# A diffusion-transformer block on one core: the MLP gate's cross-partition sum by small DMAs, and the place of two scale groups in the K stage

## The chip, the cores and the metric

The kernel runs on one core of a Trainium2 chip. The metric is the device time of one execution in microseconds; the median of five runs is compared. One execution was taken with the hardware profiler, and its trace is what the views below are read from. Engines are named as in the profile: PE is TensorE's matmul, PEld its weight load, DVE is VectorE, ACT ScalarE, POOL GpSimd, SP the engine that issues most of the loads.

## The reference

One block of a diffusion transformer for x of shape (2, 256, 1152), in bfloat16, with a conditioning vector c per batch. Six vectors of 1152 elements per batch are made from c: shift, scale and gate for the attention half, and the same for the MLP half.

```
mod = (silu(c) @ w_mod).reshape(B, 6, 1, D)
shift_a, scale_a, gate_a, shift_m, scale_m, gate_m = mod[:, 0..5]
h   = layernorm(x) * (1 + scale_a) + shift_a
q, k, v from h @ wqkv, 2 heads of 576
a   = softmax(q k^T / sqrt(576)) v @ wo
x   = x + gate_a * a
h2  = layernorm(x) * (1 + scale_m) + shift_m
m   = gelu(h2 @ w_fc1) @ w_fc2          # 1152 -> 4608 -> 1152
out = x + gate_m * m
```

## The kernel before

The 512 tokens (2 batches of 256) are the free dimension of most matmuls, and D = 1152 is cut into KD = 9 chunks of 128 partitions, F = 4608 into KF = 36. All engines run their instructions in the order of the program: the last lines of the kernel chain the instructions of each engine in that order, so a step's place in the text is its place in the engine's queue. Weights stream in by large DMAs from SP into five wide buffers, and each is released when its last reader is done.

**K stage.** The keys come first. The modulated input hT0 is made chunk by chunk: `scale_group(k0, k1)` multiplies columns of w_scale_a with silu(c) on PE (line 250, tile pm), `scale_add` adds one on VectorE (line 260), `transpose_x` turns a chunk of the normalised input over on PE (line 267, tile pt), and `both` (line 319) multiplies the chunk with its scale: batch 0 on VectorE (line 273), batch 1 on ScalarE (line 274). `k_step(k, c0, c1, m0, m1)` then adds chunk k to the accumulators of panels m0 to m1 of six panels of K (line 282), for token columns c0 to c1. w_scale_a is loaded in five pieces (line 109), interleaved with pieces of w_k (line 106): chunks 0-1, 2-3, 4-5, 6-7 and 8. The loop from chunk 3 on (lines 400 to 409) does, at k = 3 and k = 5, the first three panels of step k, then the scale group of the next two chunks, then the transposes of chunk k + 1, and then the other panels of step k. Steps 4 and 6 go in two halves of 256 tokens, batch 0 first. The two PSUM buffers of tag aux hold pm and pt in turn. After the K stage come the other three K panels, shift_a, the q panels, scores and softmax, V, the attention product, the output projection with gate_a, and the second layernorm.

**The MLP gate.** gate_m is needed only at the very end, as a row broadcast to all partitions. `gate_vector` makes it on VectorE while PE runs fc1: after panel 22, VectorE multiplies each of the nine chunks of w_gate_m with silu(c) (lines 472 and 474), and adds them up in part, 128 partitions by 1152 per batch. What is left is a sum over the 128 partitions. VectorE transposes in blocks of 32 by 32 (line 481) and sums each block along the free dimension (line 482): folded holds, for each of the four quadrants of 32 partitions, the sum of that quadrant. The sum over the four quadrants goes by matmul: `gate_vector_finish` (line 488), called behind panel 34, multiplies folded with fold, a constant of four stacked identities, in float32, one matmul per batch (line 492, tile pg; four instructions in the profile). VectorE casts the result (line 494), POOL writes it to a DRAM scratch (line 496), and reads it back broadcast over the partitions (`broadcast_gate`, line 461).

**fc1 and fc2.** fc1 has 36 panels: the first 12 in halves of 256 tokens, the others with nine matmuls of 512 columns each (line 751), with a Gelu on ScalarE behind each (lines 772 and 783). fc2 follows with thirteen groups of 36 matmuls (line 807), most of 384 columns, in a pool of six PSUM accumulators. Behind each group VectorE multiplies with gate_m (line 813), POOL (in the last group VectorE) adds the residual (line 815), and SP stores the output (line 818).

Of the kernel before, what the change touches and what calls it, by code (L numbers as in the profile page):

```python
# [8 lines left out]
FP32 = mybir.dt.float32  # L9
BF16 = mybir.dt.bfloat16  # L10
ACT = mybir.ActivationFunctionType
ALU = mybir.AluOpType
AX = mybir.AxisListType
# [6 lines left out]
def kernel(  # L20
# [11 lines left out]
    nc = tc.nc  # L32
    B, N, D = x.shape
# [3 lines left out]
    P = 128  # L37
    T = B * N
# [3 lines left out]
    KF = F // P  # L42
# [10 lines left out]
    const = ctx.enter_context(tc.tile_pool(name="const", bufs=1))  # L53
    act = ctx.enter_context(tc.tile_pool(name="act", bufs=1))
    wide = ctx.enter_context(tc.tile_pool(name="wide", bufs=5))
    work = ctx.enter_context(tc.tile_pool(name="work", bufs=2))
    small = ctx.enter_context(tc.tile_pool(name="small", bufs=4))
    psum = ctx.enter_context(tc.tile_pool(name="psum", bufs=2, space=PSUM))

    def acc_tile(shape, name, dt=FP32):  # L60
        return psum.tile(shape, dt, name=name, tag="acc", bufs=6)

    def aux_tile(shape, name, dt=FP32):
        return psum.tile(shape, dt, name=name, tag="aux", bufs=2)
# [27 lines left out]
    ident = const.tile([P, P], BF16, name="ident")  # L92
# [26 lines left out]
    def load_rows(name, view, col0):  # L119
        w = wide_tile(name)  # L120
        for r in range(0, KD, 3):
            load = nc.sync.dma_start(w[:, r:r + 3, :], view[:, r:r + 3, col0:col0 + D])
            first_load.setdefault(name, load.ins)
        return w
# [118 lines left out]
    def scale_group(k0, k1, tile_of=aux_tile, pm=None):  # L243
        if pm is None:
            pm = tile_of([P, k1 - k0, B], "pm")
        for j in range(k0, k1):
            if j == 0:
                nc.tensor.matmul(pm[:, 0, :], ones_row[:], ones_row[:, 0:B], start=True, stop=False)
            for k in range(KD):
                nc.tensor.matmul(  # L250
                    pm[:, j - k0, :], w_scale_a[:, k, j * P:(j + 1) * P], sT[:, k, 0:B],
                    start=(k == 0 and j > 0), stop=(k == KD - 1),
                )
        return pm

    def scale_add(pm, k0, k1, eng="d"):
        if eng == "a":
            nc.scalar.activation(scale_a[:, k0:k1, :], pm[:], ACT.Identity, bias=ones[:])
        else:
            nc.vector.tensor_scalar_add(scale_a[:, k0:k1, :], pm[:], 1.0)  # L260

    def transpose_x(ks, ts, pt=None, j0=0):
        if pt is None:
            pt = aux_tile([P, len(ks), len(ts) * P], "pt", BF16)
        for j, t in enumerate(ts, j0):
            for i, k in enumerate(ks):
                nc.tensor.transpose(pt[:, i, j * P:(j + 1) * P], xns[t][:, k * P:(k + 1) * P], ident[:])  # L267
        return pt
# [9 lines left out]
    def k_step(k, c0=0, c1=T, m0=0, m1=KM1):  # L278
        for m in range(m0, m1):
            if k == 0 and c0 == 0:  # L280
                pk[m] = acc_tile([P, T], "pk")
            nc.tensor.matmul(  # L282
                pk[m][:, c0:c1], w_k[:, k, m * P:(m + 1) * P], hT0[:, k, c0:c1],
                start=(k == 0 and c0 == 0), stop=(k == KD - 1), skip_group_check=True,
            )
# [33 lines left out]
    def both(pt, k):  # L319
        for b, e in enumerate("da"):  # L320
            modulate(pt, 0, k, b, b * N, e)
# [76 lines left out]
    k_step(2, 0, N)  # L398
    k_step(2, N, T)
    for k in range(3, KD):  # L400
        split = 3 if k in (3, 5) else 0
        k_step(k, 0, T, 0, split)
        if k in (3, 5, 7):
            k1 = min(k + 3, KD)
            scale_add(scale_group(k + 1, k1), k + 1, k1)
        if k < KD - 1:
            both(transpose_x([k + 1], range(NT)), k + 1)
        for c0, c1 in ((0, N), (N, T)) if k in (4, 6) else ((0, T),):
            k_step(k, c0, c1, split)
    for m in range(KM1):  # L410
        k_evac(m)

# [38 lines left out]

    s32 = const.tile([P, KD, B], FP32, name="s32")
    nc.vector.tensor_copy(s32[:], sT[:, :, 0:B])
    fold = const.tile([P, 32], FP32, name="fold")
    nc.vector.tensor_reduce(fold[:], ident[:].rearrange("p (q a) -> p a q", a=32), axis=AX.X, op=ALU.add)
    gates_dram = tc.dram_tile([2, B, D], BF16, name="gates_dram")

    def broadcast_gate(g):
        gate = act.tile([P, B, D], BF16, name="gate", tag="gate")
        for b in range(B):  # L460
            nc.gpsimd.dma_start(gate[:, b, :], gates_dram[g, b:b + 1, :].partition_broadcast(P))
        return gate
# [3 lines left out]
    def gate_vector(g, wg):  # L466
        part = act.tile([P, B, D], FP32, name="part", tag="x_sb")
        folded = small.tile([P, B, D // 32], FP32, name="folded", tag="folded", bufs=1)
        for k in range(KD):
            for b in range(B):  # L470
                if k == 0:
                    nc.vector.tensor_scalar_mul(part[:, b, :], wg[:, k, :], s32[:, k, b:b + 1])  # L472
                else:
                    nc.vector.scalar_tensor_tensor(  # L474
                        part[:, b, :], wg[:, k, :], s32[:, k, b:b + 1], part[:, b, :],
                        op0=ALU.mult, op1=ALU.add,
                    )
        for b in range(B):
            for c in range(0, D, PW):
                blocks = work.tile([P, PW // 32, 32], FP32, name="tmp", tag="tmp", bufs=3)  # L480
                nc.vector.transpose(blocks[:].rearrange("p j r -> p (j r)"), part[:, b, c:c + PW])
                nc.vector.tensor_reduce(
                    folded[:, b, c // 32:(c + PW) // 32], blocks[:], axis=AX.X, op=ALU.add
                )

        return lambda: gate_vector_finish(g, folded)

    def gate_vector_finish(g, folded):
        rows = D // 32
        pg = aux_tile([rows, B, 32], "pg")  # L490
        for b in range(B):
            nc.tensor.matmul(pg[:, b, :], folded[:, b, :], fold[:], start=True, stop=True)
        nat = work.tile([rows, B, 32], BF16, name="nat_v", tag="nat_v", bufs=1)
        nc.vector.tensor_copy(nat[:], pg[:])  # L494
        for b in range(B):
            nc.gpsimd.dma_start(gates_dram[g, b, :].rearrange("(j r) -> j r", r=32), nat[:, b, :])  # L496
        return broadcast_gate(g)

    def gate_natural(g, wg):
# [130 lines left out]
    w_gate_m = load_rows("w_gate_m", wmod_v, S_GATE_M * D)  # L630
# [106 lines left out]
    def load_f2(j):  # L737
        w = wide.tile([P, 27, PW], BF16, name=f"w_f2_{j}", tag="wide")
        i = 27 * j
        while i < 27 * (j + 1):  # L740
            n, kk = divmod(i, KF)
            cnt = min(KF - kk, 27 * (j + 1) - i)
            nc.sync.dma_start(w[:, i - 27 * j:i - 27 * j + cnt, :], wfc2_v[:, kk:kk + cnt, n * PW:(n + 1) * PW])
            i += cnt
        w_f2.append(w)
# [3 lines left out]
    def f1_mm(dst, m, k, c0, c1, start, **kw):  # L749
        ml = m % KD  # L750
        nc.tensor.matmul(  # L751
            dst, w_f1[m // KD][:, k, ml * P:(ml + 1) * P], hT[:, k, c0:c1],
            start=start, stop=(k == KD - 1), **kw,
        )
# [23 lines left out]
    gate_m = None  # L778
    for m in range(MSPLIT, KF):
        pacc = acc_tile([P, T], "pacc")  # L780
        for k in range(KD):
            f1_mm(pacc[:], m, k, 0, T, k == 0)
        nc.scalar.activation(gT[:, m, :], pacc[:], ACT.Gelu_apprx_tanh)  # L783
        if m == 22:
            gate_m_finish = gate_vector(1, w_gate_m)
        if m == KF - 2:
            gate_m = gate_m_finish()
        if m == MSPLIT:
            load_f2(0)
        if m > MSPLIT and m % KD == KD - 1:  # L790
            load_f2(m // KD)
# [9 lines left out]
    for gi, (n, t, c0, cw) in enumerate(groups):  # L801
        b = t // TPB
        last = gi == len(groups) - 1
        pacc = acc_tile([P, cw], "pacc")
        for kk in range(KF):
            j, r = divmod(n * KF + kk, 27)
# [3 lines left out]
                start=(kk == 0), stop=(kk == KF - 1),  # L810
# [51 lines left out]
```

## Time and profile before

| | |
|---|---|
| median of five runs | 243.28 us (242.82 to 243.54) |
| the profiled execution's own time | 243.54 us |
| its span | 241.8 us |
| granted TensorE clock | 1.0 |
| PE busy | 235.1 us, 97% of the span |
| DVE, ACT, POOL busy | 91.5, 60.2, 28.3 us |
| share of the chain that ended last | PE 94%, DMA 3% |

The span is the time from the first to the last instruction in the trace; the time of an execution is 1.74 us longer. In the timeline, each line gives start and duration in microseconds, the engine, the line of the kernel, the operation, output and input tiles, shapes and the number of instructions merged; in brackets stands how long the engine was idle before, and what ended the idle time. In the chain that ended last, each line gives start, duration, engine, tile, line and number of instructions. A few per cent of the matmul records can be missing from a trace, so a count may be short by one.

### The profile page before, as it was taken

The page shows a single profiled execution, that of the slowest core. Times are in us where ns is not written, and L with a number is a line of the kernel's source. Part 1 is how long each engine was busy: PE and PEld are TensorE (multiplying, and loading weights), DVE is VectorE, ACT ScalarE, POOL GpSimd, SP SyncE. Part 2 cuts the span into 40 slices and gives each one's busy share as a digit, 9 for nine tenths or more (in the row PEclk, how much of TensorE's full clock was granted, in tenths as well). Part 3 has the DMA queues.
Part 4 walks back from the last instruction along what each step waited for, and adds up shares of the span by engine and source line. Part 5 has one row for each costly group of instructions (what it writes and reads, how often), then busy time and mean ns, then how long its engine had stood idle before and what let it go on. Part 6 is the DMA issues. An engine that isn't in the chain of part 4 may idle for free.

```text
span 241.8 us, 4006 instructions
## 1 busy us (share of the span) xinstructions
PE 235.1 (97%) x1699; PEld 145.4 (60%) x1710; DVE 91.5 (38%) x194; ACT 60.2 (25%) x122; POOL 28.3 (12%) x47
## 2 busy tenths in 40 slices
PE   8699999999999999999999999999999999999994
PEld 5577444466657666888844444444665666656674
DVE  4752442319325678831002999950010000000001
ACT  6723322307215032671422333322000000000000
POOL 2300000002300324100000000001121111111111
DMA  6999999996599993739999999999200000000000
GB/s 219 322 315 320 376 368 393 389 391 215 120 325 394 392 276 77 195 59 364 389 393 390 340 327 282 281 327 278 98 16 19 18 16 16 19 18 17 28 23 16
DMA packets 48925, 53.30 MB, mean 220 GB/s; under 512 B 9731, under 2 KB 36619, under 8 KB 48907
## 3 DMA queue, kind: packets, MB, share of 16 engines
q1 hardware_dynamic: 41312, 50.14, 62.1%
q10 hardware_dynamic: 7083, 1.72, 4.5%
q0 software_dynamic: 512, 1.19, 1.7%
q8 instruction: 13, 0.21, 0.4%
q14 instruction: 5, 0.04, 0.0%
HBM read 50.15 MB, written 1.19 MB: 212 GB/s over the span
## 4 chain that ended last, share of the span: by engine, by line
PE 94%; DMA 3%; SPq 1%; issue 0%; DVE 0%; DVEq 0%
PE pacc L807 29%; PE pacc L751 29%; PE pacc L698 7%; PE pacc L604 7%; PE pq L526 7%; PE pk L282 5%; DMA w_scale_a<-in_w_mod_dram 3%; PE pk L311 2%; PE pa L645 2%; PE ps_s L561 2%; PE pn L421 2%; PE pm L250 1%; SPq L88 1%; PE pt L267 1%; PE pg L503 0%
## 5 line engine op out<-in xcount | busy, mean ns | idle before, releaser
L751 PE MATMUL pacc<-hT,w_f 128*128 128x256 bf16 (+1 forms) x427 | 70.3, 325 | 0.3
L807 PE MATMUL pacc<-w_f,gT 128*128 128x384 bf16 (+2 forms) x468 | 70.5, 314 | 0.0
L807 PEld LDWEIGHTS <-gT 128*128 128x128 bf16 x468 | 44.4, 98 | 26.2
L751 PEld LDWEIGHTS <-w_f 128*128 128x128 bf16 x432 | 42.2, 98 | 27.6
L813 DVE TENSOR_TENSOR tmp<-pacc,gate 128x384 f32<-128x384 f32 (+2 forms) x13 | 6.9, 527 | 65.6 <-PE pacc L807 57.2
L783 ACT ACTIVATE gT<-pacc 128x512 bf16<-128x512 f32 x24 | 14.3, 597 | 32.6 <-PE pacc L751 32.6
L474 DVE SCALAR_TENSOR_TENSOR part<-w_gate_m,s,part 128x1152 f32<-128x1152 bf16 x16 | 21.4, 1415 | 0.0
L815 POOL TENSOR_TENSOR o_sb<-tmp,x 128x384 bf16<-128x384 f32 (+1 forms) x12 | 11.7, 973 | 53.8 <-DVE tmp L813 53.8
L698 PE MATMUL pacc<-w_o,big 128*128 128x384 bf16 x108 | 17.9, 326 | 0.0
L526 PE MATMUL pq<-hT,w_q 128*128 128x512 bf16 x79 | 17.7, 379 | 0.1
L604 PE MATMUL pacc<-w_v,hT 128*128 128x384 bf16 x108 | 17.7, 326 | 0.0
L604 PEld LDWEIGHTS <-hT 128*128 128x128 bf16 x108 | 10.5, 98 | 7.1 <-issue 0.3
L698 PEld LDWEIGHTS <-big 128*128 128x128 bf16 x108 | 10.4, 98 | 7.2 <-issue 0.4
L526 PEld LDWEIGHTS <-w_q 128*128 128x128 bf16 x81 | 7.8, 98 | 9.4
L282 PE MATMUL pk<-big,w_k 128*128 128x256 bf16 (+1 forms) x82 | 12.9, 301 | 0.1
L704 POOL TENSOR_TENSOR x<-tmp,x_sb 128x384 f32<-128x384 f32 x8 | 7.3, 914 | 27.1 <-DMA w_scale_m<-in_w_mod_dram 15.2
L472 DVE TENSOR_SCALAR part<-w_gate_m,s 128x1152 f32<-128x1152 bf16 x2 | 1.6, 818 | 22.1 <-DMA w_gate_m<-in_w_mod_dram 22.1
L282 PEld LDWEIGHTS <-w_k 128*128 128x128 bf16 x84 | 7.9, 97 | 2.5 <-issue 0.2
L496 POOL DMA_DIRECT2D gates_dram<-nat_v x2 | 1.1, 536 | 67.7 <-DVE nat_v L494 67.7
L772 ACT ACTIVATE gT<-pacc 128x512 bf16<-128x512 f32 x12 | 6.5, 598 | 9.1 <-PE pacc L751 9.1
L517 POOL DMA_DIRECT2D gates_dram<-nat x4 | 2.3, 582 | 49.0 <-DVE nat L514 48.4
L703 DVE TENSOR_TENSOR tmp<-pacc,gate 128x384 f32<-128x384 f32 x12 | 6.6, 549 | 3.1 <-PE pacc L698 3.1
(106 smaller groups left out, 163.6 us busy)
## 6 DMA issues: line engine op xcount, KB each, us to landing
w_f<-in_w_fc_dram SPq DMA_DIRECT2D x12, 864.0 KB, 14.3
w_f<-in_w_fc_dram SPq DMA_DIRECT2D x3, 1728.0 KB, 9.9
w_f<-in_w_fc_dram SPq DMA_DIRECT2D x2, 2592.0 KB, 17.9
w_gate_a<-in_w_mod_dram SPq DMA_DIRECT2D x3, 864.0 KB, 12.8
w_v<-in_wqkv_dram SPq DMA_DIRECT2D x3, 864.0 KB, 13.8
w_o<-in_wo_dram SPq DMA_DIRECT2D x3, 864.0 KB, 13.9
w_shift_m<-in_w_mod_dram SPq DMA_DIRECT2D x3, 864.0 KB, 8.3
w_scale_m<-in_w_mod_dram SPq DMA_DIRECT2D x3, 864.0 KB, 15.1
```

The costliest lines, as they stand in the source:

```text
L282: nc.tensor.matmul(pk[m][:, c0:c1], w_k[:, k, m * P:(m + 1) * P], hT0[:, k, c0:c1], start=(k == 0 and c0 == 0), stop=(k == KD - 1), skip_g ...
L474: nc.vector.scalar_tensor_tensor(part[:, b, :], wg[:, k, :], s32[:, k, b:b + 1], part[:, b, :], op0=ALU.mult, op1=ALU.add,)
L526: nc.tensor.matmul(pq[m][:], w_q[:, k, m * P:(m + 1) * P], hT[:, k, :], start=(k == 0), stop=(k == KD - 1), skip_group_check=True,)
L604: nc.tensor.matmul(pacc[:], hT[:, k, t * P:(t + 1) * P], w_v[:, k, pnl * PW:(pnl + 1) * PW], start=(k == 0), stop=(k == KD - 1),)
L698: nc.tensor.matmul(pacc[:], aT[:, k, t * P:(t + 1) * P], w_o[:, k, c0:c1], start=(k == 0), stop=(k == KD - 1),)
L703: nc.vector.tensor_tensor(tmp[:], pacc[:], gate_a[:, b, c0:c1], op=ALU.mult)
L704: (nc.gpsimd if pool_add else nc.vector).tensor_tensor(x1[:, t, c0:c1], tmp[:], x_sb[:, t, c0:c1], op=ALU.add)
L751: nc.tensor.matmul(dst, w_f1[m // KD][:, k, ml * P:(ml + 1) * P], hT[:, k, c0:c1], start=start, stop=(k == KD - 1), **kw,)
L783: nc.scalar.activation(gT[:, m, :], pacc[:], ACT.Gelu_apprx_tanh)
L807: nc.tensor.matmul(pacc[:], gT[:, kk, t * P:(t + 1) * P], w_f2[j][:, r, c0 - n * PW:c0 - n * PW + cw], start=(kk == 0), stop=(kk == KF - 1),)
L813: nc.vector.tensor_tensor(tmp[:], pacc[:], gate_m[:, b, c0:c0 + cw], op=ALU.mult)
L815: (nc.vector if last else nc.gpsimd).tensor_tensor(o_sb[:], tmp[:], x1[:, t, c0:c0 + cw], op=ALU.add)
```

## The change

Two places are edited. In the K stage the scale groups of chunks 4-5 and 6-7 come behind two panels of steps 3 and 5 instead of three, and steps 4 and 6 go in full width, 512 tokens, instead of two halves. In the MLP gate, the sum over the four quadrants leaves PE: four DMAs from POOL lay the four quadrants of folded side by side in the free dimension of 32 partitions (quads), VectorE adds them (total), turns the result in 32-by-32 blocks (turned) and casts it (nat), and two DMAs write it to the DRAM scratch. `gate_vector_finish` and the constant fold are gone, and the whole gate follows panel 22 in one go, where the second part had waited for panel 34.

```diff
@@ K stage @@
-        split = 3 if k in (3, 5) else 0
+        split = 2 if k in (3, 5) else 0
         k_step(k, 0, T, 0, split)
         if k in (3, 5, 7):
             k1 = min(k + 3, KD)
             scale_add(scale_group(k + 1, k1), k + 1, k1)
         if k < KD - 1:
             both(transpose_x([k + 1], range(NT)), k + 1)
-        for c0, c1 in ((0, N), (N, T)) if k in (4, 6) else ((0, T),):
-            k_step(k, c0, c1, split)
+        k_step(k, 0, T, split)
@@ gate @@
-    fold = const.tile([P, 32], FP32, name="fold")
-    nc.vector.tensor_reduce(fold[:], ident[:].rearrange("p (q a) -> p a q", a=32), axis=AX.X, op=ALU.add)
...
-        return lambda: gate_vector_finish(g, folded)
-
-    def gate_vector_finish(g, folded):
         rows = D // 32
-        pg = aux_tile([rows, B, 32], "pg")
-        for b in range(B):
-            nc.tensor.matmul(pg[:, b, :], folded[:, b, :], fold[:], start=True, stop=True)
-        nat = work.tile([rows, B, 32], BF16, name="nat_v", tag="nat_v", bufs=1)
-        nc.vector.tensor_copy(nat[:], pg[:])
-        for b in range(B):
-            nc.gpsimd.dma_start(gates_dram[g, b, :].rearrange("(j r) -> j r", r=32), nat[:, b, :])
+        quads = small.tile([32, P // 32, B * rows], FP32, name="quads", tag="quads", bufs=1)
+        for a in range(P // 32):
+            nc.gpsimd.dma_start(quads[:, a, :], folded[32 * a:32 * (a + 1), :, :].rearrange("p b j -> p (b j)"))
+        total = small.tile([32, 96], FP32, name="total", tag="total", bufs=1)
+        nc.vector.memset(total[:], 0.0)
+        nc.vector.tensor_reduce(
+            total[:, 0:B * rows], quads[:].rearrange("p a c -> p c a"), axis=AX.X, op=ALU.add,
+        )
+        turned = small.tile([32, 96], FP32, name="turned", tag="turned", bufs=1)
+        nc.vector.transpose(turned[:], total[:])
+        nat = small.tile([32, 96], BF16, name="nat_v", tag="nat_v", bufs=1)
+        nc.vector.tensor_copy(nat[:], turned[:])
+        flat = gates_dram[g, :, :].rearrange("b (j r) -> (b j) r", r=32)
+        nc.gpsimd.dma_start(
+            flat[0:64, :].rearrange("(q c) r -> c q r", q=2), nat[:, 0:64].rearrange("c (q r) -> c q r", q=2),
+        )
+        nc.gpsimd.dma_start(flat[64:B * rows, :], nat[0:B * rows - 64, 64:96])
         return broadcast_gate(g)
@@ behind the fc1 panels @@
         if m == 22:
-            gate_m_finish = gate_vector(1, w_gate_m)
-        if m == KF - 2:
-            gate_m = gate_m_finish()
+            gate_m = gate_vector(1, w_gate_m)
```

## The prediction

> **What bounds the kernel.** I read the busy shares first, then the chain that ended last in order of time, then the timeline round the two edited places.
>
> ```profile
> PE 235.1 (97%) x1699; PEld 145.4 (60%) x1710; DVE 91.5 (38%) x194; ACT 60.2 (25%) x122; POOL 28.3 (12%) x47
> ```
>
> TensorE is busy for 97% of the span, and the list of what PE waited for holds nothing after 9.98 us but three short waits of the start. So from there on the time is a sum over PE's queue: an edit counts by the PE time that it takes out, or by the gap that it opens. The chain says what the first edited place, the gate between the fc1 panels, takes there:
>
> ```profile
> 164.83 1.24 PE pacc L751 x5
> 166.07 0.26 PE pg L492 x4
> 166.32 2.05 PE pacc L751 x9
> 168.37 70.31 PE pacc L807 x468
> ```
>
> Four float32 matmuls stand between panel 34 and panel 35, on the path itself. VectorE had its part done long before, and what follows the matmuls ends late, on other engines:
>
> ```profile
> 160.28 0.55 DVE L482 TENSOR_REDUCE folded<-tmp 128x12 f32<-128x384 f32 x1
> ...
> 166.36 0.22 DVE L494 CAST nat_v<-pg 36x64 bf16<-36x64 f32 x1 [5.52 <-PE pg L492]
> ...
> 175.02 0.56 DVE L813 TENSOR_TENSOR tmp<-pacc,gate 128x384 f32<-128x384 f32 x1 [8.44 <-DMA gate<-gates_dram]
> ```
>
> (timeline of VectorE: its last sum is done at 160.83, and the cast then waits 5.52 us for pg.) The second place is the K stage, in the timeline: weight loads, a matmul, then VectorE and ScalarE, with the scale group's weights read at 16.15 and ScalarE behind VectorE.
>
> ```profile
> 15.92 0.10 PEld L282 LDWEIGHTS <-w_k 128*128 128x128 bf16 x1
> 16.15 0.32 PEld L250 LDWEIGHTS <-w_scale_a 128*128 128x128 bf16 x3
> ...
> 16.35 0.19 PE L250 MATMUL pm<-sT,w_scale_a 128*128 128x2 bf16 x2
> ...
> 17.25 0.35 DVE L273 TENSOR_SCALAR big<-pt,scale_a 128x256 bf16<-128x256 bf16 x1
> ...
> 17.63 0.47 ACT L274 ACTIVATE big<-pt,scale_a 128x256 bf16<-128x256 bf16 x1 [2.74 <-DVE big L273]
> ```
>
> **Edit 1, the gate's matmuls go.** Two ways to measure them. From 166.07 to 168.37 PE spent 2.30 us on panel 35 and the four matmuls; a panel is nine matmuls of 512 columns, 10.79/50 = 0.216 us each (49 with one record missing in 10.74, and 0.05 beside it), so 1.94 us; 2.30 - 1.94 = 0.36. The Gelu of panels 33, 34 and 35 begins at 164.16, 166.10 and 168.41: steps of 1.94 and 2.31, difference 0.37. Lower bound: the 0.26 that the chain shows for pg itself; upper bound: the 0.42 us that the weight loads stood idle before pg. I take -0.36, both direct rows.
>
> **Edit 1, what comes in.** Everything new runs on POOL, VectorE and DMA queues; no PE instruction waits for it. Folded is complete at 160.83. Four POOL issues of 0.54 us (row: two nat_v issues in 1.07), and a landing 3.7 us after the last issue begins (row: 2.2 KB each to gates_dram; bounds 2.0, the gates_dram writes near 58 us, and 9.9, the 864 KB load of that stretch, since the weight loads still fill the DMA engines until about 168.5): 160.9 + 3 x 0.54 + 3.7 = 166.2. On VectorE a memset, reduce, transpose and copy of at most 96 columns, none dearer than the 0.55 reduce and the 0.22 copy: about 1.2, so 167.4. Two more writes to gates_dram, 0.54 + 3.7: 171.6. Two broadcasts at 3.6 after issue: about 175.3 for batch 0 (bounds 170 and 195 if each of the three steps takes 2.0 or 9.9). Before it was 175.0. The first user is the multiplication of fc2's first group, whose sums are ready near 168.4 + 36 x 0.150 = 173.8 (0.150 = 70.31/468). The accumulator pool has six buffers, so PE runs on until six groups are full, near 168.4 + 6 x 5.4 = 200.8: even the late bound has cover. Queued behind the new waits are only, on VectorE, that same multiplication, and on POOL the additions that follow it. SP is not passed by anything; the output stores come after the additions. The last fc2 weight load is under way when the four DMAs start; 128 rows of 288 bytes are 37 KB, 0.1 us at the 326 GB/s shown there, and it feeds the third column panel, 43 us later. Cost: 0. The removed fold reduction (0.36 us at 33.30) stood on VectorE beside PE's q panels: 0.
>
> One rule speaks against putting a sum on DMAs: the Trainium skill, "DMA: Bandwidth & Descriptors", section "Anatomy of one DMA", gives each such transfer a nearly constant 2.0 us however small, and asks for large batches. The row says 3.7 us in this stretch, more than the rule. With 2.0 for each of the three steps the gate would land near 170, by the row near 175; the end of the kernel would be the same by either.
>
> **Edit 2, whole width in place of halves.** In steps 4 and 6 twelve matmuls of 256 columns become six of 512. The chain has twelve halves of step 6 in 1.31 us and twelve full ones of steps 7 and 8 in 2.59, so 1.295 per six: -0.015 a step, -0.03 for both.
>
> **Edit 2, the scale groups come one panel earlier.** Groups 4-5 and 6-7 stand behind two panels instead of three, so PE wants them 0.216 us earlier; the third panel is done later, so PE's sum is unchanged unless a weight is late. Group 4-5's load is issued at 8.67 and lands 7.4 later (the DMA issues of that window): 16.07 +- 0.05. The weight load began at 16.15; each one begins about 0.02 after the matmul before it, here 16.13, so before there was no wait, with little to spare. After, it wants to begin at 15.93, cannot before about 16.12 (0.05 after landing, as at 9.93 to 9.98), and takes 0.10: pm then begins at 16.22-16.25 instead of 16.13. A new gap of +0.10. Bounds: 0, if the load lands 0.15 earlier, and 0.216, the whole shift, if it lands later in both kernels alike. Group 6-7 is issued at 11.91 and lands 7.2 later, 19.11, where PE wants it after 19.42: no wait.
>
> **Edit 2, the cover of the modulation.** Step 4 in halves needs VectorE's half only, and ScalarE's 0.65 us later; in full width its first matmul needs both. From the end of the transposes (17.18 in the chain): VectorE begins 0.07 later, takes 0.35, ScalarE follows 0.03 later with 0.47: 0.92, and with 0.06 to hand over 0.98. PE's cover after: four panels, 0.86, and the next transposes, 0.22: 1.08. Spare 0.10 in step 4 and as much in step 6. Cost 0; bounds 0 and, with no cover for ScalarE's part at all, 0.47 at each. I take 0 because both rows run alike at 17.63 and 21.13.
>
> **Sum.** -0.36 - 0.03 + 0.10 = -0.29 us. The profiled execution took 243.54 (span 241.8 and 1.74 round it), the highest of the five runs; its span would become 241.5. The difference is applied to the median, 243.28: **242.99**, -0.12%. That is inside 0.2% (0.49 us), about what a measurement of this kernel can tell from no change.
>
> **Rivals.** *All gain, no wait:* the scale load lands earlier beside the same PE work, and pg costs its upper bound: -0.42 - 0.03 = -0.45, 242.83. For it: landings move with HBM traffic, and 0.15 us decides. Against: 16.07 sits behind the wanted 15.93.
> *ScalarE uncovered:* the full-width steps wait for ScalarE. Its rows show that it starts only after VectorE's half, 0.03 behind, so any delay there goes straight on. Place: first matmul of steps 4 and 6. It costs from 0.10 of delay on, turns the sum positive from 0.25 of delay (two gaps of 0.15), and passes +0.2% from 0.49 (two gaps of 0.39). With ScalarE's 0.47 bare at both places: 0.94 - 0.29 = +0.65, 243.93. Against: both places show spare time.
> *It does not do what it says:* the 0.36 is not pg's, but a hand-over that another step of panel 35 would show too; then only the K stage is left, +0.07 to +0.19, 243.4. Against: the other panels step by 1.94 without it.
>
> **From these to numbers.** Forecast 0.55, all gain 0.25, ScalarE 0.12, no effect 0.08. The five runs spread by 0.72, so a median can move by some 0.2: of the forecast a fifth passes -0.49, of all gain about half; ScalarE passes +0.49 in most cases. Faster 0.25, same 0.65, slower 0.10. The range: the cases' bounds from -0.45 to the no-effect case's +0.19, widened by the scatter downward and by 0.1 upward, 242.5 to 243.6; ScalarE's case is mostly left out.
>
> **What would show it.** After: no pg in the chain, the last Gelu step 1.94; a gap at pm of group 4-5 put down to the w_scale_a DMA, 0.05 to 0.2; no gap before steps 4 and 6; the gate's multiplication near 175 without a PE gap. A wait of PE for ScalarE in the K stage, or any PE gap in fc2, would prove me wrong.

## The result and the profile after

The change takes 242.99 us in the median of 29 runs (242.45 to 243.68), beside 243.32 for the kernel before in 51 runs on the same chips (242.82 to 244.15). The ratio is 0.9986 with a 95% interval of 0.9979 to 0.9992: 0.34 us faster, 0.19 to 0.51. The prediction was -0.29 and a time of 242.99. The total is inside the forecast, and its interval reaches to the 0.2% (0.49 us) that the text named as the bound. Two terms of the sum were wrong and offset each other, as shown below.

The profiled execution after the change took 242.57 us, with a span of 240.8. That is 1.0 below the span before, three times the measured gain, because 0.67 us of it is the first scale matmul's start (9.98 before, 9.31 after: the first weight load landed 6.6 us after its issue in place of 7.4). So the two traces are compared by stretches of PE's chain, not by their spans.

The busy shares, from the page of the kernel after:

```profile
PE 234.9 (98%) x1683; PEld 144.2 (60%) x1694; DVE 92.2 (38%) x196; ACT 60.1 (25%) x122; POOL 30.3 (13%) x51
```

The chain that ended last, in order of time (start, duration, engine, tile, line, count), from the middle of panel 34 to the end of fc2:

```profile
164.16 0.05 issue
164.22 3.19 PE pacc L755 x14
167.40 70.30 PE pacc L809 x468
```

There is no pg any more. The chain enters fc1 at 97.20 and fc2 at 167.40, 70.20 us, where it took 97.81 to 168.37, 70.56, before: -0.36. Each of the last five Gelu steps is 1.94 or 1.95.

The gate itself, on VectorE and on POOL in the timeline (start, duration; in brackets the idle time before and what ended it):

```profile
167.45 0.63 DVE L489 TENSOR_REDUCE total<-quads 32x72 f32<-32x288 f32 x1 [7.29 <-DMA quads<-folded]
168.12 0.27 DVE L493 STREAM_TRANSPOSE turned<-total 32x96 f32<-32x96 f32 x1
168.42 0.20 DVE L495 CAST nat_v<-turned 32x96 bf16<-32x96 f32 x1
174.39 0.56 DVE L815 TENSOR_TENSOR tmp<-pacc,gate 128x384 f32<-128x384 f32 x1 [5.78 <-DMA gate<-gates_dram]
```

```profile
160.36 2.01 POOL L486 DMA_DIRECT2D quads<-folded  x4 [61.80 <-DVE total L488]
168.91 0.55 POOL L497 DMA_DIRECT2D gates_dram<-nat_v  x1 [6.53 <-DVE nat_v L495]
```

VectorE waits 7.29 us for the four small DMAs, POOL waits 6.53 us for VectorE's result, and PE waits for neither. The first multiplication with the gate begins at 174.39, where it was 175.02; fc1 too begins 0.61 earlier in this trace, so within the kernel the gate comes no sooner than before.

The K stage after, PE and ScalarE in the timeline:

```profile
15.46 0.59 PE L250 MATMUL pm<-sT,w_scale_a 128*128 128x2 bf16 x18
15.92 0.38 PE L267 MATMUL pt<-ident,xn 128*128 128x128 bf16 x4
16.14 1.03 PE L282 MATMUL pk<-big,w_k 128*128 128x512 bf16 x4
17.00 0.39 PE L267 MATMUL pt<-ident,xn 128*128 128x128 bf16 x4
17.27 1.89 PE L282 MATMUL pk<-big,w_k 128*128 128x512 bf16 x8
```

```profile
16.75 0.47 ACT L274 ACTIVATE big<-pt,scale_a 128x256 bf16<-128x256 bf16 x1 [2.53 <-DVE big L273]
```

ScalarE ends at 17.22 and step 4's first matmul starts at 17.27, 0.27 behind the transposes at 17.00; in front of the four panels the same distance is 0.22 (15.92 to 16.14). That is a gap of 0.05. Step 6 has its like (20.53 to 20.81, ScalarE from 20.28 to 20.75). No wait is listed against PE for either; they are only seen by comparing starts.

The weight load of group 4-5 did wait for its DMA:

```profile
15.32 0.64 PEld L250 LDWEIGHTS <-w_scale_a 128*128 128x128 bf16 x18 [0.19 <-DMA w_scale_a<-in_w_mod_dram]
```

It began 0.14 ahead of its matmul at 15.46, where before it began 0.20 ahead (16.15 and 16.35), and the matmul was not late for it.

### The profile page after: what moved, and what is told of

Its sections match the earlier page's. It is cut to its first block, busy times and chain, and to the rows that moved or that the text cites. A ratio compares the mean times of both kernels' runs of the same rounds, so it can differ in the third digit from the quotient of the medians.

```text
span 240.8 us, 3982 instructions
## 1 busy us (share of the span) xinstructions
PE 234.9 (98%) x1683; PEld 144.2 (60%) x1694; DVE 92.2 (38%) x196; ACT 60.1 (25%) x122; POOL 30.3 (13%) x51
## 4 chain that ended last, share of the span: by engine, by line
PE 95%; DVE 2%; DMA 1%; issue 0%; SPq 0%; DVEq 0%
PE pacc L809 29%; PE pacc L755 29%; PE pacc L702 7%; PE pacc L608 7%; PE pq L530 7%; PE pk L282 5%; PE pk L311 2%; PE pa L649 2%; PE ps_s L565 2%; PE pn L420 2%; DMA x_sb<-in_x_dram 1%; DVE stats L195 1%; PE pt L267 1%; PE pm L250 1%; PE pg L507 1%
## 5 line engine op out<-in xcount | busy, mean ns | idle before, releaser
L486 POOL DMA_DIRECT2D quads<-folded x4 | 2.0, 509 | 61.8 <-DVE total L488 61.8
L282 PEld LDWEIGHTS <-w_k 128*128 128x128 bf16 x72 | 6.8, 97 | 3.5 <-issue 0.2
```

The lines of the kernel that those rows point to most:

```text
L282: nc.tensor.matmul(pk[m][:, c0:c1], w_k[:, k, m * P:(m + 1) * P], hT0[:, k, c0:c1], start=(k == 0 and c0 == 0), stop=(k == KD - 1), skip_g ...
```

## Experiments

**The gate alone.** The changed kernel with the K stage of before:

```diff
-        split = 2 if k in (3, 5) else 0
+        split = 3 if k in (3, 5) else 0
...
-        k_step(k, 0, T, split)
+        for c0, c1 in ((0, N), (N, T)) if k in (4, 6) else ((0, T),):
+            k_step(k, c0, c1, split)
```

> The gate's new form alone, the K stage as before (three panels ahead of the scale groups, steps 4 and 6 in halves). If four float32 matmuls cost PE 0.36 us: 0.36 below before, ratio 0.9985, fc1 from its first matmul to fc2's first in 70.20 us in place of 70.56, and the K stage as before. If the 0.36 is a hand-over of panel 35 that stays when pg goes: ratio 1.000 and a Gelu step of 2.31 in front of the last.

Ratio 0.9974 (0.9961 to 0.9987). From the chain that ended last:

```profile
97.67 70.20 PE pacc L756 x432
167.87 70.30 PE pacc L810 x468
```

70.20 us for fc1, as with the whole change, and the K stage is as before. The -0.36 belongs to pg; the rival in which the cost stays is out, by the trace and by an interval that excludes 1. The timed gain is 0.63 us (0.32 to 0.95): the trace's 0.36 is inside the interval, near its lower end.

**The K stage alone.** Before, with the other part of the diff:

```diff
-        split = 3 if k in (3, 5) else 0
+        split = 2 if k in (3, 5) else 0
...
-        for c0, c1 in ((0, N), (N, T)) if k in (4, 6) else ((0, T),):
-            k_step(k, c0, c1, split)
+        k_step(k, 0, T, split)
```

> The K stage's new order alone, the gate by float32 matmuls. The prediction says +0.07 us, from a gap of 0.10 where the scale group of chunks 4-5 waits for its weights and no gap ahead of steps 4 and 6. The profile after the change suggests the other source: no lost time at the scale group, and about 0.05 each ahead of steps 4 and 6, where the full-width matmul begins 0.05 after ScalarE's half is done; sum +0.07 too. The ratio is 1.0003 by both, so the timeline decides: pt to pk 0.27 in place of 0.22 says ScalarE, pm more than 0.22 after the last panel's matmul says the load.

Ratio 1.0000 (0.9985 to 1.0015), which can't tell +0.07 from 0. The timeline of PE:

```profile
17.21 0.39 PE L267 MATMUL pt<-ident,xn 128*128 128x128 bf16 x4
17.48 1.89 PE L282 MATMUL pk<-big,w_k 128*128 128x512 bf16 x8
19.74 0.60 PE L250 MATMUL pm<-sT,w_scale_a 128*128 128x2 bf16 x18 [0.37 <-DMA w_scale_a<-in_w_mod_dram]
20.20 0.38 PE L267 MATMUL pt<-ident,xn 128*128 128x128 bf16 x4
20.42 1.03 PE L282 MATMUL pk<-big,w_k 128*128 128x512 bf16 x4
21.28 0.39 PE L267 MATMUL pt<-ident,xn 128*128 128x128 bf16 x4
21.56 1.46 PE L282 MATMUL pk<-big,w_k 128*128 128x512 bf16 x6
```

The distance from transposes to step is 0.27 and 0.28 again, so ScalarE's gap is there with either gate. And in this execution PE did wait for a load, not at group 4-5 but at group 6-7. The bracket says 0.37 us, counted from the modelled end of the matmul before it. By starts it is 0.53: from 17.48 to 19.74 pm comes 2.26 behind step 4, where after the change it comes 1.73 behind it (17.27 to 19.00). The load took 8.3 us from issue to landing here, and 7.2 before and after the change. PE lost nothing at group 4-5 in this trace or in the one after the change. The load wait is real and moves from run to run. It is not of the new order alone: in the run with bfloat16 weights of 128 columns, below, whose K stage is that of before, the same load took 8.3 us too, and pm came 2.24 behind step 4 in place of 1.96, a wait of 0.28. With the load that late, the new order waits 0.25 more, about the panel by which its group comes earlier.

**Three panels and full width.** Before, with steps 4 and 6 in full width only (the second half of the diff above):

> Before, but with steps 4 and 6 in full width, the scale groups still behind three panels. PE's cover is one panel (0.216) shorter than in the change. If ScalarE's half sets the start of the full-width steps, the gap grows from 0.05 to 0.27 at each: +0.54 - 0.03 = +0.5 us, ratio 1.002. If the cover had 0.10 to spare, as predicted, it is short by 0.12 at each: +0.2, ratio 1.0009. If only the load matters: -0.03.

The timeline of PE:

```profile
17.26 0.39 PE L267 MATMUL pt<-ident,xn 128*128 128x128 bf16 x4
17.75 2.10 PE L282 MATMUL pk<-big,w_k 128*128 128x512 bf16 x9
```

0.49 from transposes to step 4 (and 21.01 to 21.50 at step 6) in place of 0.22: a gap of 0.27 at each, and the chain that ended last goes through VectorE and ScalarE there. One panel less of cover makes each gap 0.22 longer than with two panels, one panel's time, so nothing is to spare. From the first long stretch of step matmuls to the last twelve, the chain takes 9.93 us (13.48 to 23.41), where before it took 9.43 (13.89 to 23.32). The timed ratio is 1.0004 (0.9990 to 1.0018), 0.44 us at most, a little less than the 0.5 of the trace; why is not settled.

**Both halves on VectorE.** The changed kernel, where the modulation for steps 4 and 6 stays on one engine:

```diff
-    def both(pt, k):
-        for b, e in enumerate("da"):
+    def both(pt, k, engines="da"):
+        for b, e in enumerate(engines):
...
-            both(transpose_x([k + 1], range(NT)), k + 1)
+            both(transpose_x([k + 1], range(NT)), k + 1, "dd" if k + 1 in (4, 6) else "da")
```

> The change, with both halves of the modulation for steps 4 and 6 on VectorE (0.35 + 0.35 us one after the other, in place of 0.35 on VectorE and then 0.47 on ScalarE). If ScalarE's half sets the start of steps 4 and 6, which costs 0.05 at each, that half is ready 0.12 earlier and both gaps close: pt to pk 0.22 again, 0.10 less than the change in the K stage, ratio to before 0.9981. If the gaps have another cause they stay at 0.27.

The timeline of PE:

```profile
16.96 0.39 PE L267 MATMUL pt<-ident,xn 128*128 128x128 bf16 x4
17.18 1.89 PE L282 MATMUL pk<-big,w_k 128*128 128x512 bf16 x8
...
20.45 0.39 PE L267 MATMUL pt<-ident,xn 128*128 128x128 bf16 x4
20.67 1.46 PE L282 MATMUL pk<-big,w_k 128*128 128x512 bf16 x6
```

From transposes to step it is 0.22 at both: the gaps are closed. The same stretch of the chain as above takes 9.39 us (13.18 to 22.57), 9.49 with the change (13.22 to 22.71), 9.43 before. So the two gaps cost 0.10, the halves 0.04, and in these two traces the load costs nothing. fc1 is at 70.20. By the chain this kernel is 0.40 below before; timed it is 0.9986 (0.9973 to 1.0000), which the runs can't tell from the change's own.

**More work in the K stage.** Before, with the transposes of chunk 4 done six times:

```diff
-            both(transpose_x([k + 1], range(NT)), k + 1)
+            turned_x = transpose_x([k + 1], range(NT))
+            for _ in range(5 if k == 3 else 0):
+                transpose_x([k + 1], range(NT), turned_x)
+            both(turned_x, k + 1)
```

> Before, with the four transposes of chunk 4 done six times over in the K stage, about 1.1 us more PE work ahead of the scale group of chunks 6-7 and of shift_a. If PE alone sets the K stage's time in every execution, the whole 1.1 us shows: ratio 1.0045. If in a part of the executions PE waits for the load stream there (scale group 6-7 in one profile, shift_a in another), the work fills that wait and less shows: ratio 1.001 to 1.003.

The stretch of the chain takes 10.54 us (13.35 to 23.89), +1.11; the ratio is 1.0039 (1.0024 to 1.0053), +0.95 of the 1.11, with the whole of it inside the interval. So the K stage's PE time does show in the end; load waits hide half of it at most (the low end of the interval is 0.58 us). The same amount of work in fc1, behind all loads, was not measured, so the 0.95 has no yardstick beside it.

**pg twice.** Before, with each matmul of pg issued again:

```diff
-        for b in range(B):
+        for b in [*range(B), *range(B)]:
             nc.tensor.matmul(pg[:, b, :], folded[:, b, :], fold[:], start=True, stop=True)
```

> Before with the two float32 matmuls of the gate issued twice (the second pair overwrites the first). It prices pg by itself: four more instructions, +0.26 if a pair costs what the chain shows for it and the rest of 0.36 is the change between data types, +0.36 if the whole cost repeats, 0 if pg costs nothing. Ratio 1.0011 to 1.0015, or 1.000.

Ratio 1.0012 (0.9998 to 1.0027). The chain:

```profile
166.90 0.40 PE pg L492 x8
167.30 2.05 PE pacc L751 x9
169.35 70.30 PE pacc L807 x468
```

From panel 34's end to fc2 2.45 us, 0.15 more than before's 2.30. Less than either expectation: an instruction more costs 0.04, and 0.21 of the 0.36 is paid once, however many there are. By starts in the trace of before, 0.10 of it lies ahead of the first of them (0.31 from panel 34's last matmul at 165.69 to pg at 166.00, where a step is 0.216) and the rest behind it, up to panel 35's first matmul at 166.26.

**What the once-paid part is.** Three kernels with another pg, one run each, read by their traces and not by their times. First bfloat16 in place of float32, which makes two instructions of four:

```diff
-    fold = const.tile([P, 32], FP32, name="fold")
+    fold = const.tile([P, 32], BF16, name="fold")
...
+        low = small.tile([P, B, D // 32], BF16, name="folded_bf", tag="folded_bf", bufs=1)
+        nc.vector.tensor_copy(low[:], folded[:])
```

> Before, with the gate's fold matmuls in bfloat16 in place of float32 (folded rounded to bfloat16 on VectorE, two matmul instructions in place of four). pg twice showed that four more float32 instructions cost 0.15, so 0.21 of the 0.36 is paid once. If that once-paid part belongs to float32 (the weight load cannot run ahead, 0.42 idle before it), bfloat16 costs 0.1 or less: panel 34's end to fc2 2.0 us. If any narrow matmul here pays it, 0.25 to 0.3: 2.2 us.

Then the same with weights of 128 columns (a zeroed tile [P, B, P], the 36 sums copied into its first columns):

> The bfloat16 fold matmuls with weights of all 128 columns (36 of sums, the rest zero) in place of 36 columns. The bfloat16 pair costs 0.26, of which only 0.05 goes by the number of instructions (0.15 for four more in float32). If the once-paid 0.21 comes from the narrow weights, which did not load ahead of the panel's last matmul (0.42 idle before them), full-width weights load ahead and the cost falls to 0.15 or less: panel 34's end to fc2 below 2.1 us. If it comes from the short matmul or the change of tile, it stays at 0.25.

And float32 with weights of 128 columns:

> The float32 fold matmuls, four instructions as before, with weights padded to 128 columns. In bfloat16 the padding took the cost from 0.26 to 0.05. If the width alone decides whether the weights load ahead, float32 falls from 0.36 to about 0.15 (four instructions at 0.04): panel 34's end to fc2 2.1 us. If float32 weights do not load ahead whatever their width, it stays at 0.36 or more.

The weight loads in the timeline, narrow bfloat16, wide bfloat16 (with its matmuls) and wide float32 in turn, one fence for each kernel:

```profile
165.50 0.12 PEld L496 LDWEIGHTS <-folded_bf 128*36 128x36 bf16 x2 [0.42 <-issue]
```

```profile
165.70 0.31 PEld L497 LDWEIGHTS <-folded_bf 128*128 128x128 bf16 x2
165.91 0.20 PE L497 MATMUL pg<-fold,folded_bf 128*128 128x32 bf16 x2
```

```profile
165.63 0.63 PEld L495 LDWEIGHTS pg<-fold,folded_w 128*128 128x128 f32 x4
```

Panel 34's end to fc2 takes 2.20 (165.57 to 167.77), 1.99 (166.08 to 168.07) and 2.31 us (166.01 to 168.32). Less 1.94 for the panel, pg costs 0.26, 0.05 and 0.37, beside 0.36 before. The narrow weights wait out the last matmul (0.42 idle, in bfloat16 as in float32); the wide ones load 0.21 ahead of their own matmul and the idle time is gone. So the once-paid part goes with the narrow weights. In float32 the padding gains nothing all the same: four loads take 0.63, 0.16 each, in place of 0.21 for four narrow ones, which is about what loading ahead gained; the third expectation, 0.15, missed by that. The trace of before has the same sign elsewhere: the loads of 32 columns for pn (line 421) stand idle for 0.42 us behind matmuls of 512 columns, at 29.72 and at 37.69, with no releaser shown. Loads of 128 columns but only 64 rows (line 561, at 54.20) have 0.21 us of it behind matmuls of 256 columns. So it may be the change of shape and not the number of columns that counts; no run separates the two, and why such weights do not load ahead, no trace shows.

**A gate that comes late.** The change, with passes on VectorE between the quadrant sums and total:

```diff
+        for _ in range(36):
+            nc.vector.tensor_scalar_mul(part[:, 0, :], part[:, 0, :], 1.0)
         rows = D // 32
```

> The change, with 36 further passes over 1152 float32 elements on VectorE between the quadrant sums and the addition of the four quads (their result is read by nobody), some 20 to 45 us. If the six accumulators cover a late gate up to about 200 us in the span, as predicted, and the passes take 0.8 us each, the gate lands near 196, the first multiplications run late one after the other, PE has no gap in fc2, and the time is that of the change, 243.0. If the gate's time matters earlier than that: 245 or more.

The same with 60 passes:

> The same with 60 passes. If the cover ends when six groups are full, near 200 us, and the gate lands G us into the span (about 216 with 0.8 us a pass), PE stands still for about G - 200, and the time is 243 plus that, near 258. If the cover is longer or PE does not wait for the accumulators: 243.

With 36, VectorE and the chain show:

```profile
195.83 1.49 DVE L817 TENSOR_TENSOR tmp<-pacc,gate 128x384 f32<-128x384 f32 x3 [5.83 <-DMA gate<-gates_dram]
```

```profile
167.36 70.31 PE pacc L811 x468
```

The gate is 21 us later than in the change, fc2 takes its 70.31 all the same, and the one run took 242.55 us. With 60 passes the first multiplication begins at 215.27, and PE stops:

```profile
215.88 6.33 PE L811 MATMUL pacc<-w_f,gT 128*128 128x384 bf16 x24 [13.34 <-DVE tmp L817]
```

That run took 258.38 us. So the cover is there and ends where the sixth accumulator is full, at 202.54 (215.88 - 13.34), where PE's idle time begins.

## Why the prediction was right, and where it was wrong

*Edit 1, what goes:* right, -0.36 in the trace after and with the gate alone. It was a sum of 0.21 that goes with narrow weights that do not load ahead and 0.15 for four instructions, which the prediction did not part. The upper bound, the 0.42 idle, was not what it cost: part of it is the last matmul itself.

*Edit 1, what comes in:* right at 0. The steps were off and nearly made up for one another: the addition of the four quads began at 167.45, where the text had them landed at 166.2 (the median of the four is 5.3 us after issue, not 3.7, with the weight load still running), and the two writes to the scratch, with the weight load over, took 1.6 in place of 3.7. The gate was 0.9 earlier than the 175.3 of the text, of which 0.6 is the earlier start of the whole trace. The 2.0 us that the Trainium skill, "DMA: Bandwidth & Descriptors", section "Anatomy of one DMA", gives for a small DMA stands between these two rows. The late-gate runs confirm why none of it counts; the end of cover is 202.5 and not 200.8, because a full group takes 36 x 0.1625 = 5.85 us and the mean over all 468 matmuls mixed in two narrower groups; in that trace fc2 begins at 167.4, and 167.4 + 6 x 5.85 = 202.5.

*Edit 2, whole width:* -0.03 predicted, -0.04 in the kernel where both gaps are closed.

*Edit 2, the groups one panel earlier:* the wait exists, but not as a fixed +0.10. In the trace after the change the weight load of group 4-5 stood idle for 0.19 us for the DMA, and its matmul was not late for it. With the K stage alone PE waited at group 6-7, 0.53 by starts. The landing was taken from one trace to 0.05 us, while it moves by more than that between executions (7.2 to 8.3 us after issue for group 6-7); the bounds of 0 to 0.216 held for group 4-5, and group 6-7, put at no wait, went beyond them.

*Edit 2, the cover of the modulation:* this step failed. It said 1.08 of cover against 0.98 of need, 0.10 to spare and a cost of 0; the traces show 0.05 missing at each step. By the prediction's own sign (a wait of PE for ScalarE in the K stage would prove it wrong) its account of the K stage is wrong, though the time came out. The mistake lies in where the cover was counted from. It was counted from the transposes' end in the chain, 17.18, up to where PE would end its panels, but a matmul starts as soon as the one before lets it, some 0.16 ahead of that modelled end (records of four transposes last 0.38, and the next matmul starts after 0.22), as the timeline of PE before shows:

```profile
16.80 0.38 PE L267 MATMUL pt<-ident,xn 128*128 128x128 bf16 x4
17.02 0.81 PE L282 MATMUL pk<-big,w_k 128*128 128x512 bf16 x3
```

From starts alone: transposes at 16.80, then 0.22 + 0.86 + 0.22 gives 18.10 for step 4 with two panels ahead of the group; ScalarE ended at 17.63 + 0.47 = 18.10, and 0.05 to hand over, as in the trace after (17.22 to 17.27; the prediction had 0.06), makes 18.15. That sum gives the 0.05, out of rows that were there before. The rival *ScalarE uncovered* thus named the right place and was priced at its upper end.

*The sum:* -0.36 - 0.04 + 0.10 = -0.30 in the chains, against -0.34 (0.19 to 0.51 faster) timed. The +0.10 was put on the load, which cost nothing in the trace after, and came from ScalarE, which was put at 0: the total was right in part by luck. The times alone can't show either term; the K stage alone is timed at 1.0000, within 0.37 us either way.

## What to carry to other kernels

On a kernel bound by one engine's queue, take covers and needs from starts of instructions; an end that the profile models can be late by more than the margin that is argued about. Here the four tiny matmuls between large ones cost more by weights that do not load ahead (0.21) than by their number (0.15), so look for idle time of the weight loads in front of such matmuls; either padding them to 128 columns in bfloat16 (0.05 in place of 0.26) or taking them off PE worked. Small DMAs, slow as they are, cost nothing here as long as the buffers behind the bound engine covered them, and the cover can be counted: six accumulators of 5.85 us.

## What the runs showed that was not expected

Behind the 13.34 us of standstill PE did not come back at full speed. In the run with 60 passes its granted clock is 1.00 up to 206 us, 0.94 from 206 to 207, 0.50 from there to 220.5, past the end of the standstill, and 1.00 again from 221 on. The mean of 0.94 puts the fall near 206.9, some 4.3 us after PE stopped at 202.54. The weight loads after the gap start 0.32 us apart for the first matmuls of 384 columns, twice the 0.1625 of the others:

```profile
216.16 0.15 PEld L811 LDWEIGHTS <-gT 128*128 128x128 bf16 x1 [0.17 <-issue]
216.48 0.15 PEld L811 LDWEIGHTS <-gT 128*128 128x128 bf16 x1 [0.17 <-issue]
```

The run is 15.8 us longer than the one with 36 passes, 2.5 more than the standstill. The slow steps last from 215.88 to 220.32, 14 loads in 4.4 us, which is 2.2 us more than 14 steps of 0.1625; from there on they are short again. The Trainium skill, "TensorE: Matmul & The Clock Gate", Part 1 on the clock gate, says that TensorE falls to half its clock after some 3.4 us without work and comes back after about as long a time of work. The factor of two agrees with this trace; here the fall came after about 4.3 us and the way back took 4.4 us or a little more. No other run of this case has an idle stretch of that length.
